# Merging the inverse in 64-row quadrants, moving the E products, and leading with the last channels

## The chip, the cores and the metric

The kernel runs on one core of a Trainium2 chip. The metric is the device time of one launch in microseconds. It was run seven times: median 1137.3 us, lowest 1134.52, highest 1139.42.

## What is computed

Two blocks in a row. The first is a linear recurrence over 768 tokens for 4 sequences of 8 heads, each head with a 40 by 40 state:

```python
for t in range(S):
    y[:, :, t] = einsum('bhd,bhde->bhe', rt, state)
    Sa = einsum('bhde,bhe->bhd', state, at)
    state = state * wt[:, :, None, :] - einsum('bhd,bhe->bhde', Sa, bt)
    state = state + einsum('bhd,bhe->bhde', vt, kt)
```

Its output, as 3072 tokens of 320 channels, goes through four experts that all tokens use. `p` is `domain_probs` divided by its row sum:

```python
for e in range(4):
    h = maximum(x @ w1[e], 0)            # 320 -> 1024
    out += p[:, e:e + 1] * (h @ w2[e])   # 1024 -> 320
```

All data are 32-bit floats.

## The kernel before

**The recurrence** is worked in chunks of 64 tokens. A *unit* is one chunk of two of the four sequences, so there are 12 x 2 = 24 units, and a tile holds the two sequences on its two halves of 64 partitions. Inside a unit the recurrence becomes a triangular system: `F` (L478) and `E` (L483) are products of the decayed keys with themselves, and the inverse of the identity minus the causal part of `F` is needed. The kernel inverts diagonal blocks of 32 by 32 (`substitute`, L511: VectorE turns the blocks into `M` and prepares them, GpSimd runs the substitution into `Z`), and `merge` (L563) joins the blocks into the 64 by 64 inverse `QT`: `pY` (L583) multiplies the block below the diagonal with one inverse, `pQ` (L595) multiplies the result with the other inverse, and ScalarE copies the sums from PSUM back (L589, L600). Both are written head by head with 32 x 32 tiles of TensorE: 16 matmuls each, for the quarters 1 and 3 or 0 and 2 of the partitions.

`within(q)` (L384) is a generator that makes everything of a unit that needs no state: decays `G` (transposes `pg`), tokens `NT` and `KT` (transposes `pNT`, `pKT`), causal scores `pc`, `F` and `E` (`pfe`: the F products and the E products stand in one pair of PSUM banks), `ET` (VectorE's causal copy of E, L493) and `pev`, the product of E with V, which ScalarE copies to `EV` (L504). `step(q)` (L603) does what needs the state: `prn`, `psat` (the product with the inverse `QT`, and its transpose), `pxr`, `pdy`. Nearly all of these are 64 x 64 quadrants of TensorE made by `quadrants` (L365), so they show as line 371. A 32-bit matmul is two weight loads and two matmuls in the trace, so a product of 16 matmuls is 32 matmul instructions.

**The experts** run on chunks of 256 tokens. `up` (L718) first multiplies the last 64 of the 320 channels with 64 x 64 tiles (L727, 8 matmuls of 256 columns), and then the first 256 channels with the full 128 x 128 array (L735, 8 matmuls). The second layer is a Strassen-like scheme of products (L842, 160 columns) over sums of tiles (`add_h`, L836, VectorE), and VectorE adds the scaled products to the output (L753). The pieces of `w1` stream in over the SP queue (L282).

**The order** of the work is written by hand in the loop at L1022, one turn for each unit `u`: the generators of unit u + 1's merge (`m`) and step (`s_next`), of the running step (`s`), and of the `within` of units u + 1 and u + 2 (`w_next`, `w`) are advanced a yield at a time, and `gap(n)` puts one or two pieces of the experts (from the list `todo`) between them as filler for TensorE. Turns with u < 5 are called early and have an order of their own. The TensorE stream of a late turn is, with the tile size in brackets: `pY` [32], L727 [64], L735 and L842 [128], `pQ` [32], F and E products `pfe`, `psat`, L727 [64], L735 and L842 [128], `pev`, `pxr`, L727 [64], L735, L842 and `pg` [128], `pdy`, L727 [64], L735, L842, `pNT`, `pKT` [128], `pc`, `prn` [64], and `pY` of the next unit.

**PSUM:** products of the recurrence take one bank at a time from five in turn (`big`, L72); the experts take from three (`mm`): two for the `ph` of an `up`, one for each product of the second layer. A bank is free again when its last reader is done.

Of the kernel before, what the change touches and what calls it, by code (L numbers as in the profile page):

```python
# [15 lines left out]
def kernel(  # L16
# [114 lines left out]
    def kept(name, shape, n, value=0.0, eng=nc.gpsimd, lo=0):  # L131
        tiles = []
        for i in range(n):
            t = const.tile(shape, FP32, name=f"{name}{i}")
            eng.memset(t[:, :, lo:shape[2]], value)
            tiles.append(t)
        turn = [0]

        def take():
            turn[0] += 1  # L140
            return tiles[(turn[0] - 1) % n]

        return take
# [15 lines left out]
    ETs = kept("ET", of_64, 1)  # L159
    EVs = kept("EV", of_64, 1, lo=D)  # L160
    QTs = kept("QT", of_64, 1)
    RHs = kept("RH", of_64, 1, lo=D)
    state = [kept(f"state{i}_", [P, NJ, 64], 1)() for i in range(B)]


    class Unit:
        pass
# [3 lines left out]
    def begin(u):  # L171
        q = Unit()
        q.u, q.c, q.bp = u, u // (B // 2), u % (B // 2)
        q.b = [2 * q.bp, 2 * q.bp + 1]
        q.start, q.end = q.c == 0, q.c == NC - 1
        q.n = {}
        units.append(q)
        return q
# [143 lines left out]
    def of_slot(x, s):  # L322

        return x.rearrange("p (j s) e -> p j s e", s=2)[:, :, s, :]
# [59 lines left out]
    def within(q):  # L384
# [93 lines left out]
        pf = quadrants(p, 0, BY_TOKENS, L, lambda j, s, i: (  # L478
            s, i ^ s, j, of_slots(q.AT, s, j, i), of_pairs(NT, s, j, i),
        ))  # L480
        if q.u == 0:
            p = banks("pe")
        pe = quadrants(p, NJ * L, BY_TOKENS, L, lambda j, s, i: (  # L483
            s, i, j, of_pairs(KT, s, j, i), of_slots(q.AT, s, j, i),
        ))
        q.F = sb.tile([P, H, L], FP32, name="F", tag="F", bufs=2)
        for s in range(2):
            nc.scalar.copy(out=of_slot(q.F[:], s), in_=pf[s])
        yield

        ET = ETs()
        for s in range(2):
# [18 lines left out]
    def substitute(q, eng, between=None):  # L511

        blocks = sb.tile([P, H, Q], FP32, name="blocks")
        for i in range(P // Q):
            move = nc.scalar.copy if i >= 2 else nc.vector.tensor_copy
            tc.keep_in_program_order(move(out=blocks[quarter(i)], in_=q.F[quarter(i), :, quarter(i % 2)]))  # L516
        M = sb.tile([P, Q, Q], FP32, name="M")
        cols = blocks[:].rearrange("p h c -> p c h")[:, :, None, :].to_broadcast([P, Q, 4, H])
        ins = nc.vector.transpose(out=M[:], in_=cols)  # L519
# [43 lines left out]
    def merge(q):  # L563


        Qc = sb.tile([P, H, Q], FP32, name="Qc", tag="q", bufs=2)
        QTc = sb.tile([P, H, Q], FP32, name="QTc", tag="q", bufs=2)
        tc.keep_in_program_order(nc.vector.transpose(out=dealt(Qc[:]), in_=q.Z))
        tc.keep_in_program_order(
            nc.vector.transpose(  # L570
                out=QTc[:].rearrange("p h r -> p (h r)"), in_=Qc[:].rearrange("p h c -> p (h c)"),
            )
        )
        q.QT = QTs()
        for i in range(P // Q):
            ins = nc.gpsimd.tensor_copy(out=q.QT[quarter(i), :, quarter(i % 2)], in_=QTc[quarter(i)])  # L576
            tc.keep_in_program_order(ins)
        yield

        py = big("pY")  # L580
        for h in range(H):
            for i in (1, 3):
                nc.tensor.matmul(  # L583
                    out=py[quarter(i - 1), h * Q:(h + 1) * Q], lhsT=q.F[quarter(i), h, 0:Q],
                    rhs=QTc[quarter(i), h, :], start=True, stop=True,
                )
        Y = sb.tile([P, H, Q], FP32, name="Yq")
        for i in (0, 2):
            nc.scalar.copy(out=Y[quarter(i)].rearrange("p h t -> p (h t)"), in_=py[quarter(i), 0:H * Q])  # L589
        yield  # L590

        pq = big("pQ")
        for h in range(H):
            for i in (0, 2):
                nc.tensor.matmul(  # L595
                    out=pq[quarter(i), h * Q:(h + 1) * Q], lhsT=Qc[quarter(i), h, :],
                    rhs=Y[quarter(i), h, :], start=True, stop=True,
                )
        for i in (0, 2):
            nc.scalar.copy(out=q.QT[quarter(i), :, quarter(1)], in_=by(pq[quarter(i), 0:H * Q], Q))  # L600
        yield

    def step(q, xT):  # L603
# [111 lines left out]
                lo = hi  # L715
        yield

    def up(k, xT, n, width):  # L718

        w1 = pieces[k]  # L720
        h = sb.tile([P, HF, 2 * P], FP32, name="hs", tag="hs", bufs=3)
        ph = [ps.tile([P, HF // 2, n], FP32, name="ph", tag="mm", bufs=3) for _ in range(2)]

        for f in range(HF // 2):
            for c in range(2):
                for i in range(2):
                    nc.tensor.matmul(  # L727
                        out=ph[i][half(c), f, :], lhsT=w1.last[part(i), f, half(c)],
                        rhs=xT[part(i), 2, :], start=(f == 0), stop=False,
                    )  # L730
        for i in range(2):
            for f in range(HF // 2):
                for g in range(2):
                    at = i * HF // 2 + f
                    nc.tensor.matmul(  # L735
                        out=ph[i][:, f, :], lhsT=w1.main[:, g, at * P:(at + 1) * P],
                        rhs=xT[:, g, :], start=False, stop=(g == 1 and f == HF // 2 - 1),
                    )
        for i in range(2):
            nc.scalar.activation(  # L740
                out=h[:, i * HF // 2:(i + 1) * HF // 2, 0:n], in_=ph[i][:], func=ACTF.Relu,
            )
        return h

    def scale(q, e, minus=False):
        return (minus_gate if minus else gate)[:, q.c, q.bp, e:e + 1]
# [16 lines left out]
    def mixture_of_unit(q):  # L763
# [1 line left out]
        hs, at = {}, 2 * E * q.u  # L765

        def ups(e):
            hs[e] = [up(at + 2 * e + x, q.xT, P, P) for x in range(2)]
            used(at + 2 * e + 2)
            if q.u == 0 and e + 2 < E:  # L770
                load_w2(e + 2)
# [44 lines left out]
    def mixture_of_chunk(qs, xT):  # L816
# [2 lines left out]
        at = 2 * E * (qs[0].c + 1)  # L819

        def ups(e, x):
            hs[e, x] = up(at + 2 * e + x, xT, 2 * P, P)
            used(at + 2 * e + x + 1)

        def of_h(e, s, x):
            return hs[e, x][:, :, s * P:(s + 1) * P]
# [60 lines left out]

        before = last[:]
        for e in range(E):
            todo.append(lambda e=e: ups(e, 0))  # L890
            if before:
                todo.append(before[0])
                todo.append(lambda e=e: ups(e, 1))
                todo.append(lambda e=e, then=before[1]: (then(), add_h(e)))
            else:
                todo.append(lambda e=e: (ups(e, 1), add_h(e)))
            second = down_2_at_end if (qs[0].end and e == E - 1) else down_2
            before = [lambda e=e: down_1(e), lambda e=e, second=second: second(e)]
        last[:] = before
# [9 lines left out]
    def mix(n):  # L909

        for piece in todo[:n]:
            piece()
            begin_later(3 if n > 1 else 6)
        del todo[:n]

    def run(gen, n=99):
        if gen is None:
# [104 lines left out]
    for u in range(1, NU):  # L1022
# [10 lines left out]
            run(sum_ops, sums_at.get(at, 0))  # L1033
            mix((1 if at in sparse else 2) if pieces is None else pieces)

        run(w_next)
        run(s, 1)
        gap(0)


        early = u < 5
        if early:
            run(s, 1)
        run(w, 1)
        run(s)
        if u == 1:
            mixture_of_unit(q)
# [28 lines left out]
        if not soon:  # L1076
            run(w, 1)
        if not early:
            run(s_next, 1)
        if not soon and u + 2 < NU:  # L1080
            substitute(units[u + 2], nc.gpsimd)
        run(w, 1)
        if u + 3 < NU:
            ws.append(within(units[u + 3]))
            run(ws[u + 3], 1)
# [41 lines left out]
```

## Time and profile before

| | |
|---|---|
| runs | median 1137.3 us of 7 (1134.52 to 1139.42) |
| the profiled execution's own time | 1134.52 us, of which its span is 1132.7 us |
| TensorE matmul, weight load busy | 96%, 85% of the span |
| VectorE, GpSimd, ScalarE busy | 67%, 42%, 30% |
| 16 DMA engines | 102 GB/s read and written over the span |
| granted TensorE clock | 0.95 up to 260 us, 1.00 from there on |
| TensorE busy in 0 to 260, 260 to 1005, 1005 to 1132.7 us | 229.4 of 260.0, 737.6 of 745.0, 123.6 of 127.7 us |

The units run up to about 1017 us; behind that only the experts' last pieces are left. From about 260 us on the loop is regular: a turn takes 43 to 45 us, so two turns (one chunk) take 87 to 88 us. A row of the groups gives the line, engine and operation, output and input tiles, their shapes and the count; then the busy time in us and the mean of one in ns; then the idle time of the engine just before them and what ended it. "PE" is TensorE's matmul, "PEld" its weight load. [...] successive matmuls overlap, so what a group of them costs is read from the start of the group to the start of the next.

### The profile page before, as it was taken

What the parts mean: (1) busy time and instruction counts of PE and PEld (TensorE: products, weight loads), DVE (VectorE), ACT (ScalarE), POOL (GpSimd) and SP (SyncE); (2) the same over time, 40 slices, a digit from 0 to 9 for tenths busy, and PEclk for the clock granted to TensorE, in tenths of its full rate; (3) what the DMA queues carried; (4) which work ended last, traced back from release to release, by engine and by line L of the source; (5) the groups of instructions that cost most, each with busy time, mean ns of one, the idle gap of its engine ahead of it and who ended that gap; (6) DMA issues with size and microseconds to landing.
All of it is one profiled execution on the core that took longest, in us unless ns stands there. A gap on an engine that the chain in (4) does not pass through costs nothing.

```text
span 1132.7 us, 39907 instructions
## 1 busy us (share of the span) xinstructions
PE 1090.6 (96%) x16868; PEld 961.9 (85%) x16868; DVE 759.5 (67%) x1553; ACT 338.2 (30%) x860; POOL 473.8 (42%) x1221
## 2 busy tenths in 40 slices
PE   6799997999999999999999999999999999999998
PEld 5677875888888989889898898888889899888887
DVE  8766657797667768668677677577686686553343
ACT  2323332333232232342332332332322323311110
POOL 4005626672724634625526427337346346340000
PEclk8899998999999999999999999999999999999999
DMA  7784643254263454444442543543444442231330
GB/s 116 204 252 129 136 98 79 70 129 102 76 153 80 111 129 114 110 118 104 107 121 74 134 103 82 142 102 88 128 113 92 117 111 64 76 90 55 105 93 12
DMA packets 268873, 122.27 MB, mean 108 GB/s; under 512 B 213736, under 2 KB 242072, under 8 KB 268696
## 3 DMA queue, kind: packets, MB, share of 16 engines
q1 hardware_dynamic: 265416, 119.12, 42.2%
q8 instruction: 133, 2.18, 0.8%
q10 hardware_dynamic: 3280, 0.61, 0.3%
q14 instruction: 44, 0.36, 0.1%
HBM read 111.79 MB, written 3.93 MB: 102 GB/s over the span
## 4 chain that ended last, share of the span: by engine, by line
PE 81%; DVE 6%; POOL 3%; SPq 3%; DMA 2%; issue 2%; ACT 2%; DVEq 0%; ACTq 0%; POOLq 0%
PE ph L735 27%; PE p L842 27%; PE ph L727 8%; PE pdy L371 3%; POOL Z L557 2%; PE pfe L371 2%; PE psat L371 2%; PE pxr L371 2%; PE prn L371 2%; SPq L711 1%; POOL Z L544 1%; PE pQ L595 1%; PE po L776 1%; PE pY L583 1%; PE pc L371 1%
## 5 line engine op out<-in xcount | busy, mean ns | idle before, releaser
L735 PE MATMUL ph<-xT,w1p 128*128 128x256 f32 (+1 forms) x1520 | 343.9, 379 | 0.4 <-issue 0.4
L735 PEld LDWEIGHTS ph<-xT,w1p 128*128 128x128 f32 x1520 | 274.0, 190 | 68.6 <-issue 29.0
L544 POOL TENSOR_TENSOR Z<-M,Z 128x62 f32<-128x62 f32 (+7 forms) x352 | 152.4, 433 | 366.0 <-DVE M L535 340.1
L557 POOL TENSOR_TENSOR Z<-Z 128x31 f32<-128x31 f32 (+7 forms) x704 | 249.4, 354 | 55.2
L836 DVE TENSOR_TENSOR a<-hs 128x512 f32<-128x512 f32 x220 | 154.4, 719 | 115.0 <-ACT hs L740 115.0
L740 ACT ACTIVATE hs<-ph 128x512 f32<-128x512 f32 (+1 forms) x208 | 115.8, 564 | 279.8 <-PE ph L735 279.0
L842 PE MATMUL p<-sums,a 128*128 128x160 f32 x1056 | 165.1, 299 | 0.0
L753 DVE SCALAR_TENSOR_TENSOR osb<-p,gate,osb 128x320 f32<-128x320 f32 (+1 forms) x243 | 108.0, 482 | 76.4 <-PE p L842 73.6
L842 PEld LDWEIGHTS p<-sums,a 128*128 128x128 f32 x1056 | 152.9, 190 | 2.3
L727 PE MATMUL ph<-xT,w1p 64*64 64x256 f32 (+1 forms) x1520 | 111.5, 379 | 5.1 <-issue 5.1
L842 PE MATMUL p<-w,a 128*128 128x160 f32 x704 | 103.1, 299 | 0.0
L842 PE MATMUL p<-w,hs 128*128 128x160 f32 x704 | 102.9, 299 | 0.0
L842 PEld LDWEIGHTS p<-w,hs 128*128 128x128 f32 x704 | 100.3, 190 | 2.2
L842 PEld LDWEIGHTS p<-w,a 128*128 128x128 f32 x704 | 98.1, 190 | 0.2 <-ACT hs L740 0.2
L576 POOL COPY QT<-QTc 32x256 f32<-32x256 f32 x96 | 50.1, 522 | 108.5 <-DVE QTc L570 97.9
L727 PEld LDWEIGHTS ph<-xT,w1p 64*64 64x64 f32 x1520 | 62.5, 133 | 17.9 <-issue 9.7
L519 DVE STREAM_TRANSPOSE M<-blocks 128x1024 f32<-128x1024 f32 x24 | 46.9, 1956 | 24.6 <-ACT blocks L516 24.4
L414 DVE RECIPROCAL gp<-gp 128x320 f32<-128x320 f32 x24 | 51.7, 2152 | 0.8
L504 ACT COPY EV<-pev 64x160 f32<-64x160 f32 x96 | 23.4, 286 | 67.7 <-PE pev L371 67.3
L626 ACT COPY SN<-prn 128x256 f32<-128x256 f32 x44 | 15.5, 370 | 91.6 <-DVE RH L621 89.2
L371 PE MATMUL pdy<-VC,k_tok 64*64 64x104 f32 (+1 forms) x768 | 41.3, 260 | 0.1
L667 ACT COPY RS<-pxr 64x256 f32<-64x256 f32 x88 | 32.3, 367 | 29.4 <-DVE SX L382 28.6
(148 smaller groups left out, 1351.7 us busy)
## 6 DMA issues: line engine op xcount, KB each, us to landing
w1p<-in_moe_w_dram SPq DMA_DIRECT2D x95, 512.0 KB
w1p<-in_moe_w_dram SPq DMA_DIRECT2D x190, 64.0 KB
w<-in_moe_w_dram SPq DMA_DIRECT2D x4, 1280.0 KB
sums<-in_moe_w_dram SPq DMA_DIRECT2D x9, 512.0 KB
natW<-in_w_dram SPq DMA_DIRECT2D x48, 80.0 KB
natB<-in_b_dram SPq DMA_DIRECT2D x48, 80.0 KB
natK<-in_k_dram SPq DMA_DIRECT2D x48, 80.0 KB
out_dram<-osb SPq DMA_DIRECT2D x46, 80.0 KB
```

The lines of the kernel that those rows point to most:

```text
L371: nc.tensor.matmul(out=p[row][half(col), lo + at * out_cols:lo + (at + 1) * out_cols], lhsT=lhsT, rhs=rhs, start=(n == 0), stop=(n == len( ...
L414: pin(nc.vector.reciprocal(out=gp[:], in_=gp[:]))
L519: ins = nc.vector.transpose(out=M[:], in_=cols)
L544: ins = eng.tensor_tensor(out=Z[:, 1:3, 0:n, j + 1:Q], in0=M[:, j:j + 2, None, j + 1:Q].to_broadcast([P, 2, n, m]), in1=Z[:, here, 0:n, j: ...
L557: eng.tensor_tensor(out=z[:, 0], in0=z[:, 0], in1=z[:, x], op=ALU.add)
L576: ins = nc.gpsimd.tensor_copy(out=q.QT[quarter(i), :, quarter(i % 2)], in_=QTc[quarter(i)])
L727: nc.tensor.matmul(out=ph[i][half(c), f, :], lhsT=w1.last[part(i), f, half(c)], rhs=xT[part(i), 2, :], start=(f == 0), stop=False,)
L735: nc.tensor.matmul(out=ph[i][:, f, :], lhsT=w1.main[:, g, at * P:(at + 1) * P], rhs=xT[:, g, :], start=False, stop=(g == 1 and f == HF // ...
L740: nc.scalar.activation(out=h[:, i * HF // 2:(i + 1) * HF // 2, 0:n], in_=ph[i][:], func=ACTF.Relu,)
L753: nc.vector.scalar_tensor_tensor(out=to, in0=p, scalar=sc, in1=to, op0=ALU.mult, op1=ALU.add)
L836: nc.vector.tensor_tensor(out=t[:], in0=x, in1=y, op=op)
L842: nc.tensor.matmul(out=p[:, n * HD:(n + 1) * HD], lhsT=a[:, f, :], rhs=b[:, f, :], start=(f == 0), stop=(f == HF - 1),)
```

## The change

Four things are changed.

- **The merge in quadrants.** `pY` and `pQ` are made by a new function `two_heads`: for each pair of heads and each half of 64 partitions one 64 x 64 matmul of 64 columns, so 8 matmuls each in place of 16. Both halves write the same PSUM bank. Of each product only the blocks on the diagonal are wanted; ScalarE copies them, four copies of 32 x 128 elements in place of two of 32 x 256. The other blocks have to be multiplied with zeros, so the block below the diagonal is copied to a tile of its own whose other quarters stay zero (`below`, two tiles in turn, two copies on GpSimd in each unit), and `Y` becomes a tile that is kept and was zeroed once. The copies to `below` stand in GpSimd's queue ahead of the substitution.
- **E products later.** From unit 7 on (`apart`) the F products are one stretch of `within`, with banks of their own, and the E products, with two more banks, the next; `ET` and `pev` follow one stretch later each. The loop runs the rest of `w_next` only after `w`'s next part. In TensorE's stream of a late turn the E products stand where `pev` stood, ahead of `pxr`, and `pev` stands ahead of `pdy`, behind `pg`.
- **The last channels lead.** `up` is split into `up_last` (L727) and `up_main` (L735). In late turns `lead()` issues the `up_last` of the next piece ahead of `psat`, where it stood behind it.
- `F` has one buffer in place of two.

In whole, TensorE has 8208 matmuls in place of 8592.

The diff, cut:

```diff
+    Ys = kept("Yq", [P, H, Q], 1)
+    belows = kept("below", [P, H, Q], 2)
+    EARLY = 5
+        q.apart = u >= EARLY + 2
...
-        if q.u == 0:
+        def copy_F():
+            q.F = sb.tile([P, H, L], FP32, name="F", tag="F", bufs=1)
+            for s in range(2):
+                nc.scalar.copy(out=of_slot(q.F[:], s), in_=pf[s])
+
+        if q.apart:
+            copy_F()
+            yield
+        if q.apart or q.u == 0:
             p = banks("pe")
         pe = quadrants(p, NJ * L, BY_TOKENS, L, lambda j, s, i: (
             s, i, j, of_pairs(KT, s, j, i), of_slots(q.AT, s, j, i),
         ))
-        q.F = sb.tile([P, H, L], FP32, name="F", tag="F", bufs=2)
-        for s in range(2):
-            nc.scalar.copy(out=of_slot(q.F[:], s), in_=pf[s])
-        yield
+        if not q.apart:
+            copy_F()
+            yield
...
+        q.below = belows()
+        for i in (1, 3):
+            tc.keep_in_program_order(nc.gpsimd.tensor_copy(out=q.below[quarter(i)], in_=q.F[quarter(i), :, 0:Q]))
...
-        py = big("pY")
-        for h in range(H):
-            for i in (1, 3):
-                nc.tensor.matmul(
-                    out=py[quarter(i - 1), h * Q:(h + 1) * Q], lhsT=q.F[quarter(i), h, 0:Q],
-                    rhs=QTc[quarter(i), h, :], start=True, stop=True,
-                )
-        Y = sb.tile([P, H, Q], FP32, name="Yq")
-        for i in (0, 2):
-            nc.scalar.copy(out=Y[quarter(i)].rearrange("p h t -> p (h t)"), in_=py[quarter(i), 0:H * Q])
-        yield
-        pq = big("pQ")
...
+        def two_heads(name, lhsT, rhs, to):
+            p = big(name)
+            for n in range(NJ):
+                for r in range(2):
+                    nc.tensor.matmul(
+                        out=p[half(r), n * 2 * Q:(n + 1) * 2 * Q], lhsT=lhsT[half(r), 2 * n:2 * n + 2, :],
+                        rhs=rhs[half(r), 2 * n:2 * n + 2, :], start=True, stop=True,
+                    )
+            for r in range(2):
+                for y in range(2):
+                    src = p[quarter(2 * r + y), 0:H * Q].rearrange("p (n two t) -> p n two t", two=2, t=Q)[:, :, y, :]
+                    nc.scalar.copy(out=of_slot(to[quarter(2 * r)], y), in_=src)
+
+        Y = Ys()
+        two_heads("pY", q.below, QTc, Y)
+        yield
+
+        two_heads("pQ", Qc, Y, q.QT[:, :, quarter(1)])
         yield
...
-        def ups(e, x):
-            hs[e, x] = up(at + 2 * e + x, xT, 2 * P, P)
-            used(at + 2 * e + x + 1)
+        def ups(e, x):
+            k, ph = at + 2 * e + x, []
+            def lead():
+                if not ph:
+                    ph.append(up_last(k, xT, 2 * P))
+            def piece():
+                lead()
+                hs[e, x] = up_main(k, xT, 2 * P, ph[0])
+                used(k + 1)
+            piece.lead = lead
+            return piece
...
+    def lead():
+        if todo and hasattr(todo[0], "lead"):
+            todo[0].lead()
...
-        run(w_next)
+        early = u < EARLY
+        run(w_next, 99 if early else 1)
         run(s, 1)
         gap(0)
-        early = u < 5
         if early:
             run(s, 1)
         run(w, 1)
+        if not early:
+            run(w_next)
         run(s)
...
         if not early:
+            lead()
             run(s_next, 1)
         if not soon and u + 2 < NU:
             substitute(units[u + 2], nc.gpsimd)
-        run(w, 1)
+        if early:
+            run(w, 1)
```

## Prediction, made before the changed kernel was run

> **What bounds the kernel now.** I read the page first, for the engine shares.
>
> ```profile
> span 1132.7 us, 39907 instructions
> PE 1090.6 (96%) x16868; PEld 961.9 (85%) x16868; DVE 759.5 (67%) x1553; ACT 338.2 (30%) x860; POOL 473.8 (42%) x1221
> ...
> q8 instruction: 133, 2.18, 0.8%
> ...
> PE 81%; DVE 6%; POOL 3%; SPq 3%; DMA 2%; issue 2%; ACT 2%; DVEq 0%; ACTq 0%; POOLq 0%
> ```
>
> TensorE is busy 96% of the span and holds 81% of the chain that ended last: a nanosecond off its stream is a nanosecond off the end wherever it doesn't wait. Next the waits of TensorE's matmuls, in the regular part (260 to 1005 us), to see what it waits for there:
>
> ```profile
> PE ph L727 <- issue: 3.3, 3, 1.4
> PE psat L371 <- issue: 2.5, 2, 1.3
> PE pY L583 <- DVE QTc L570: 1.3, 1, 1.3
> PE ph L735 <- issue: 0.4, 1, 0.4
> ```
>
> Hardly anything waits for another engine; what idling there is carries the label "issue", for which the profile shows no cause. The chain inside 801 to 806 us has one such hole, in the middle of a product:
>
> ```profile
> 801.21 1.09 PE pfe L371 x64
> 802.30 0.80 PE psat L371 x48
> 803.10 1.14 issue
> 804.25 0.42 PE psat L371 x11
> 804.67 1.16 PE ph L727 x15
> ```
>
> Last, TensorE's timeline, for what a group costs from its start to the next start (start, then duration):
>
> ```profile
> 747.18 0.67 PE L371 MATMUL prn<-ident,state 64*64 64x64 f32 x32
> 747.78 0.69 PE L583 MATMUL pY<-QTc,F 32*32 32x32 f32 x32
> 748.40 1.09 PE L727 MATMUL ph<-xT,w1p 64*64 64x256 f32 x16
> ...
> 757.43 0.69 PE L595 MATMUL pQ<-Yq,Qc 32*32 32x32 f32 x32
> 758.05 0.69 PE L371 MATMUL pfe<-NT,AT 64*64 64x64 f32 x32
> 758.56 0.65 PE L371 MATMUL pfe<-AT,KT 64*64 64x64 f32 x32
> 759.03 0.76 PE L371 MATMUL psat<-QT,RH 64*64 64x64 f32 x30
> ```
>
> A 64-column product that follows others of the same tile size costs 0.47 us (758.56 to 759.03). Ahead of a change of tile size it costs 0.60 (`prn` to `pY`), and the first one after a change 0.51 (`pfe` at 758.05).
>
> **Part 1, the merge in quadrants.** Starts of single matmuls show how a 0.47 us product runs: 8 rounds of four tiles, a round each 58.5 ns. `two_heads` also has 8 rounds (16 instructions on two tiles), so I take 0.47 us for it. Around `pY`, `prn` to L727 is now 0.60 + 0.62 = 1.22 us; with no change of tile size it is 0.47 + 0.47 = 0.94: 0.28 saved. Around `pQ`, which comes behind 128-wide work and still changes the tile size once, `pQ` and the first `pfe` are now 0.62 + 0.51 = 1.13; afterwards 0.51 + 0.47 = 0.98: 0.15 saved (the step from 128 to 32 and that from 128 to 64 both take 229 ns between starts). So 0.43 us a unit. From the seventh `pY` (264 us) on TensorE is the bound, for 18 units: 7.8 us. In the six units ahead, `pY` starts 0.05 to 0.15 us behind the end of `QTc` in four, so the chain through substitution sets the pace, and a shorter stream only waits longer: I take 0 (bounds: 6 x 0.43 = 2.6 saved; 6 x 0.4 = 2.4 lost to the copies below).
>
> [...] `two_heads` writes both row halves to one bank. [...] The row near to it is `pY` itself: its tiles stand in two row groups and write one bank, and the trace starts them in pairs 7 ns apart, a pair each 32 ns, about half of the 58.5 ns of a 64-column round whose row tiles have banks of their own; in turns a pair would take twice that. I go by the row[...].
>
> ScalarE: a copy of 32x256 takes 363 ns (L600), one of 64x160 286 ns (L504), so 0.8 ns an element; 32x128 is estimated at 0.26 us, and four with their 25 ns gaps at 1.14 us in place of 0.75. `Y` has about 10 us of experts' work as cover. `psat` needs all four copies of `pQ`: they end about 1.88 us behind `pQ`'s start, and TensorE gets to `psat` after `pQ`, F and the leading L727 at 0.47 + 0.51 + 0.9 = 1.9 us. That is just covered; if a copy of half the size cost the full 0.36, `psat` would wait 0.4 us, 7.4 us over 18 units. I take 0.05, so 1 us.
>
> GpSimd: two copies to `below`, about 0.39 us each like L576's median. They stand ahead of the substitution, where GpSimd waits for `M` anyway (340 us over 22 units): free. Without this cover they would cost 0.8 us a unit. `pY`'s new wait for `below` ended a unit before.
>
> **Part 2, E products later.** No product is added. E takes the place of `pev` behind 128-wide work, and `pev` joins `pdy`: by the prices above the sum moves by less than 0.03 us a unit. What goes is the hole. The page has 133 instruction packets of together 2.18 MB, 16 KB each; with 34,150 TensorE instructions (two for each of 16,868 matmuls, and 414 others) that is 256 instructions a packet. Five holes (at 455.4, 542.2, 629.1, 716.6 and 804.2 us) end where TensorE has started 14,274, 17,090, 19,906, 22,722 and 25,538 instructions: exactly 2,816, eleven packets, apart, while the code around them drifts. Each ends 1.4 to 1.6 us after a packet has landed. So TensorE runs out of instructions. Packets start on average 1.7 us after TensorE has reached the point 311 instructions ahead of the block, land 1 us later and serve 1.4 us later: 311 instructions must last about 4.1 us. In the stretch `pQ`, two `pfe`, two `psat`, L727 there are 352 in 3.6 us, and where a block ends in it, TensorE stops.
>
> [...] I price by the trace: segments from `pfe` to L735 take at least 2.96 us; at 537, 626, 713, 801 and 888 us they are 1.97, 1.11, 1.93, 1.66 and 0.39 us over it, and the L735 stretch at 454 is 0.72 over the usual: 7.8 us. Afterwards that stretch has 256 instructions with a slow L727 among them (2.9 us) and 128-wide work on both sides: 311 instructions last at least 6.2 us wherever a block ends in a regular turn. All 7.8 us should go, and nothing is late next at these places. One more hole, at 321.9 us, isn't at a block's end; I leave it in (it looks like the load of `w1p`).
>
> **Part 3, the lead.** `psat` to L735 and L727 to `psat` (0.16 + 0.20 us) take the place of L727 to L735 (0.31) and a step inside one tile size (0.04): nothing. The lead's second PSUM tile waits for VectorE's second read of the product `p75` (in the unit at 801 us it ends at 800.94; the lead comes at about 801.5). Behind a late lead are queued `psat`, and behind it ScalarE's copies to `blocks`, `M` and the substitution; each 0.1 us costs 0.1. Its piece of `w1p` must have landed 1 us earlier; such waits were 2.7 us in 7 cases, all inside changes of tile size, so 0 to 2 us, I take 0.
>
> **A wait to watch.** From `psat` to the next `pY` TensorE now needs about 30.8 us, and the chain `blocks`, `M`, substitution, `QTc` 29.4 to 29.8: `pY` starts 1.0 to 1.7 us behind `QTc`. With L727 (0.9) ahead of `psat` and E and `pev` both behind it, TensorE gets there 0.6 us sooner: 0.4 to 1.1 us of cover stay.
>
> **Sum.** Profiled execution: 1134.5 - 7.8 - 7.8 + 1 = 1119.9 us, 14.6 less. The median of the runs is 2.8 us above that execution, so 1137.3 - 14.6 = 1122.7; I say 1122.5.
>
> **Rivals.**
> - *Given back at `psat` and `pY`.* Half-size copies at full price (7.4 us), or the cover of `QTc` gone: 15.6 saved, 5 to 10 back: 1127 to 1133. Against it: the slope of two copy sizes.
> - *Blocks still run out* (the change doesn't do what it says, or new alignments meet new dense stretches, as in the early units): only part 1 counts, 1129 to 1131. Against it: the 6.2 us.
> - *More than that*: the early units gain their 2.6 us too, and the holes at 321.9 and 354 us shrink: 1116 to 1119.
> - *Slower: the shared bank.* Row tiles take turns in `two_heads`: 0.94 us more a unit, in the 18 late units and the six early ones, where `pY` and `pQ` lie on the chain, 22.5 us, less 15.6: 1144. It outweighs the gain from a delay of 0.33 us a product on (48 x 0.33 = 15.8).
>
> **Chances.** Forecast, 1119 to 1126: 0.62. Given back: 0.14. Blocks still run out: 0.09. More: 0.07. Shared bank: 0.05. Nothing moves, for causes I don't see: 0.03. The range 1117 to 1131 leaves out the last two and the edges. A measurement can tell about 0.2% (2.3 us): faster 0.92, within 0.03, slower 0.05.
>
> **What would show it.** `prn` to `pY` and `pY` to L727 at 0.47 us each; two neighbouring tiles of `pY` 7 ns apart and rounds of 58 ns (117 means turns). No "issue" rows ahead of L727 or `psat` from 400 us on. ScalarE's `QT<-pQ` at 0.26 us, and no wait of `psat` for it. `pY` still waiting for nothing. Turns of about 42.6 us, all alike. I am wrong if turns alternate again by over 0.5 us, or if `psat` or `pY` shows ScalarE, VectorE or GpSimd as what ended its wait.

## The result, and the profile after

| | before | after |
|---|---|---|
| median of the runs beside one another | 1135.88 us (34 runs) | 1129.64 us (13 runs, 1125.03 to 1131.98) |
| the profiled execution, its span | 1134.52, 1132.7 us | 1132.42, 1130.2 us |
| from the seventh `pY` to the 24th | 741.06 us | 733.00 us |

The ratio is 0.9937, with a 95% interval of 0.9923 to 0.9951: faster by 0.5 to 0.8%. The time lies inside the range that was stated (1117 to 1131), but outside the forecast's own 1119 to 1126, and the gain is less than half of what was forecast (6 to 7 us, not 14.6). So the question is where the rest went. The profiled execution of after is slower than all 13 others; its regular part is used below, its early part with care.

The page after has TensorE just as busy with 768 fewer matmul instructions, and six instruction packets fewer; the chain that ended last holds less of TensorE (72%, before 81%) and more of GpSimd and "issue":

```profile
span 1130.2 us, 38551 instructions
PE 1084.5 (96%) x16100; PEld 964.8 (85%) x16100; DVE 759.0 (67%) x1553; ACT 353.5 (31%) x956; POOL 498.5 (44%) x1272
...
q8 instruction: 127, 2.08, 0.8%
...
PE 72%; POOL 7%; DVE 6%; issue 3%; ACT 2%; DMA 1%; SPq 1%; DVEq 0%; POOLq 0%
```

The waits of TensorE's matmuls from 260 to 1005 us (engine, product and line, what it waited for; total us, times, longest) have lost `psat` and `pY`. The "issue" row ahead of the last channels (L727 before, L738 now) is larger, and `hs` is new:

```profile
PE ph L738 <- issue: 4.9, 4, 2.0
PE p L873 <- ACT hs L757: 1.0, 2, 0.7
```

TensorE's timeline in a steady turn (start, duration, group) shows what the merge brings. `prn`'s last part, `pY` and L738 start 0.49 and about 0.47 us apart, where `pY` alone cost 0.62 before a change of tile size:

```profile
748.71 0.67 PE L376 MATMUL prn<-ident,state 64*64 64x64 f32 x32
749.20 0.57 PE L599 MATMUL pY<-QTc,below 64*64 64x64 f32 x14
749.56 0.43 PE L738 MATMUL ph<-xT,w1p 64*64 64x256 f32 x2
749.61 0.22 PE L599 MATMUL pY<-QTc,below 64*64 64x64 f32 x2
749.67 1.03 PE L738 MATMUL ph<-xT,w1p 64*64 64x256 f32 x14
```

**Where the time went, from the seventh to the 24th `pY` (17 turns).** I cut TensorE's stream at its changes between 128-wide and smaller tiles, take for each kind of stretch the shortest one of the regular part, and count what every other one has over it.

| | before | after | difference |
|---|---|---|---|
| shortest stretches around `pY`, `pQ`, `pxr`, `pdy`, summed over a turn | 11.84 us | 11.34 us | -0.50 a turn, -8.4 |
| stops where an instruction block ends | 7.8 us | 0 | -7.8 |
| stretches with `pQ`, F, `psat` and L727, over the least, at 275 to 420 us | 3.0 us | 7.9 us | +4.9 |
| products that wait for `hs` | 0.3 us | 4.4 us | +4.1 |
| `psat` behind the copies of `pQ` | 0 | 0.9 us | +0.9 |
| `pY` behind `QTc`, and small ones | 1.7 us | 0 | -1.7 |
| sum | | | -8.0 (measured -8.06) |

So from the seventh to the 24th `pY` 18 us were saved and 10 were given back. **The theory after this reading (A):** both savings are as large as forecast; the lead and ScalarE's longer queue give back half. Rivals: (B) the merge itself is worth less; (C) the early units, which in this profile are 6 us later, lose it; (D) the stops in the lead are instruction fetch again.

The lead's stops come at 325.49, 370.51 and 416.26 us, each behind the first two of its 16 instructions, that is at the second PSUM tile, and not at a block's end. VectorE's timeline ahead of the second stop:

```profile
364.52 0.93 DVE L228 STREAM_TRANSPOSE G<-rawW 128x256 f32<-128x256 f32 x2 [4.69 <-DMA rawW<-in_w_dram]
...
369.01 0.51 DVE L773 SCALAR_TENSOR_TENSOR osb<-p,gate,osb 128x320 f32<-128x320 f32 x1
...
370.04 0.37 DVE L773 SCALAR_TENSOR_TENSOR osb<-p,minus_gate,osb 128x160 f32<-128x160 f32 x1
```

and TensorE's:

```profile
367.94 0.59 PE L738 MATMUL ph<-xT,w1p 64*64 64x256 f32 x2
370.51 1.55 PE L738 MATMUL ph<-xT,w1p 64*64 64x256 f32 x11 [1.98 <-issue]
```

VectorE stood 4.7 us for the load of `rawW`; the second read of `p75` (`minus_gate`) is queued behind what it did late, and ends at 370.41. TensorE goes on 0.10 us later. At the other two places VectorE had stood 7.0 us for `rawW` and 3.9 us for `rawA`; the read ends at 325.39 and 416.16, and the lead goes on at 325.49 and 416.26. The seven such stops in the traces of experiments 2, 5 and 11 end 0.10 us behind that read too. So the label "issue" hid a wait for a PSUM tile.

### The profile page after: what moved, and what is told of

It is laid out like the page before. It is cut to its first block, busy times and chain, and to the rows that moved or that the text cites. A ratio compares the mean times of both kernels' runs of the same rounds, so it can differ in the third digit from the quotient of the medians.

```text
span 1130.2 us, 38551 instructions
## 1 busy us (share of the span) xinstructions
PE 1084.5 (96%) x16100; PEld 964.8 (85%) x16100; DVE 759.0 (67%) x1553; ACT 353.5 (31%) x956; POOL 498.5 (44%) x1272
## 4 chain that ended last, share of the span: by engine, by line
PE 72%; POOL 7%; DVE 6%; issue 3%; ACT 2%; DMA 1%; SPq 1%; DVEq 0%; POOLq 0%
PE p L873 25%; PE ph L752 25%; PE ph L738 7%; POOL Z L572 4%; PE pdy L376 3%; POOL Z L559 3%; PE psat L376 2%; PE po L796 2%; PE pxr L376 1%; PE prn L376 1%; DVE M L534 1%; PE pQ L599 1%; PE pfe L376 1%; PE pev L376 1%; PE pc L376 1%
## 5 line engine op out<-in xcount | busy, mean ns | idle before, releaser
L752 PE MATMUL ph<-xT,w1p 128*128 128x256 f32 (+1 forms) x1520 | 342.7, 378 | 1.7 <-issue 1.7
L752 PEld LDWEIGHTS ph<-xT,w1p 128*128 128x128 f32 x1520 | 273.4, 190 | 62.9 <-issue 25.3
L572 POOL TENSOR_TENSOR Z<-Z 128x31 f32<-128x31 f32 (+7 forms) x704 | 256.5, 364 | 55.2
L559 POOL TENSOR_TENSOR Z<-M,Z 128x62 f32<-128x62 f32 (+7 forms) x352 | 144.4, 410 | 135.5 <-DVE M L550 109.7
L531 POOL COPY below<-F 32x256 f32<-32x256 f32 x48 | 24.9, 519 | 223.0 <-ACT F L489 221.3
L738 PE MATMUL ph<-xT,w1p 64*64 64x256 f32 (+1 forms) x1520 | 110.5, 377 | 4.9 <-issue 4.9
L873 PE MATMUL p<-w,a 128*128 128x160 f32 x704 | 106.0, 301 | 1.2 <-ACT hs L757 1.0
L738 PEld LDWEIGHTS ph<-xT,w1p 64*64 64x64 f32 x1520 | 65.3, 133 | 13.6 <-issue 9.1
L583 DVE STREAM_TRANSPOSE Qc<-Z 128x256 f32<-128x256 f32 x24 | 15.1, 628 | 46.9 <-POOL Z L572 46.6
```

Source lines behind the costliest of these rows:

```text
L559: ins = eng.tensor_tensor(out=Z[:, 1:3, 0:n, j + 1:Q], in0=M[:, j:j + 2, None, j + 1:Q].to_broadcast([P, 2, n, m]), in1=Z[:, here, 0:n, j: ...
L572: eng.tensor_tensor(out=z[:, 0], in0=z[:, 0], in1=z[:, x], op=ALU.add)
L738: nc.tensor.matmul(out=ph[i][half(c), f, :], lhsT=w1.last[part(i), f, half(c)], rhs=xT[part(i), 2, :], start=(f == 0), stop=False,)
L752: nc.tensor.matmul(out=ph[i][:, f, :], lhsT=w1.main[:, g, at * P:(at + 1) * P], rhs=xT[:, g, :], start=False, stop=(g == 1 and f == HF // ...
L873: nc.tensor.matmul(out=p[:, n * HD:(n + 1) * HD], lhsT=a[:, f, :], rhs=b[:, f, :], start=(f == 0), stop=(f == HF - 1),)
```

## The experiments

Each ratio is against the kernel before, run on the same chip, with its 95% interval.

**1. The merge alone.** The kernel before with `two_heads` and `below`, and

```diff
-        q.F = sb.tile([P, H, L], FP32, name="F", tag="F", bufs=2)
+        q.F = sb.tile([P, H, L], FP32, name="F", tag="F", bufs=1)
```

> The kernel before with the merge in quadrants alone (and one buffer of F in place of two[...]). Theory A (each part is worth what was forecast in the regular part, and half of it is given back at three places: the lead, ScalarE's copies ahead of hs, the early units): the stream is 7.8 us shorter, the 'issue' holes at a block's end stay (other places), p<-w,a waits for hs 3 us in all, early units lose up to 4: 1 to 5 us less than before. Theory B (the merge itself is worth half of what was forecast, the rest is right): 4 us less, and no waits of p<-w,a for hs. Theory C (nothing given back by the merge): 7.8 us less.

1131.68 us, 0.9955 (0.9937 to 0.9972): 5.1 us less. No product waited for `hs`, against theory A, and only two stops at a block's end were left in the regular part (0.95 us at 279.6, which the profile puts down to a load of `rawV`, and 1.27 at 887.9), though nothing was done against these. What gave back here is another thing: from `pQ` to L737 takes at least 3.83 us, where the same products take 3.36 in experiment 11, because `psat` now waits for the four copies of `pQ`.

Why so few stops are left is shown in part. Two turns of before hold some 2,832 instructions, 16 more than eleven blocks, so the end of a block creeps slowly through the same dense place. Here two turns hold some 2,705, 145 more than ten blocks, and an end comes back to a place only after 14 turns (the two stops are 18,944 instructions, 74 blocks, apart). But some ends fall as late in the stretch and don't stop. That the wait of `psat` lets the fetch catch up there is not shown: experiment 11 stops at the same two ends (280 and 892 us), and its `psat` doesn't have that wait.

**2. All but the merge** (`pY` and `pQ` as before, no `below`).

> The kernel after with the old merge (16 matmuls of 32x32 tiles, two copies, no copies to below): E products later and the lead are left. Theory A: the five holes at a block's end go (7.8 us) and the lead waits at 322 to 420 us for VectorE's second read of p75 (5 to 6 us back): 2 to 3 us less than before. Theory B (the holes were worth 7.8 and the lead costs nothing): 7.8 us less than before. No p<-w,a waits for hs over 0.5 us in all, by both.

1138.32 us, 1.0004 (0.9992 to 1.0017): no gain. In its profile the block-end stops are gone and the lead stops at 325, 371 and 417 us (1415, 3997 and 2131 ns over the least), as A says; from the seventh `pY` to the 24th it needs 738.0 us, 3.1 less than before. Two turns still hold some 2,831 instructions, so here it is not another rhythm of the blocks that took the stops away. That its median is not 2 to 3 us lower isn't explained by this. Two things on record go with it: its profile has the seventh `pY` at 269.6 us (264.4 before), and its 22 runs spend 41.0 us in the median at half the granted clock, against 34.0 in before's beside them (from the mean granted clock).

**3. All but the lead**

```diff
         if not early:
-            lead()
             run(s_next, 1)
```

> The kernel after without the lead: the last channels stand behind psat again. Theory A: the three stops inside the lead at about 325, 370 and 416 us (1.3, 2.0 and 1.1 us, 7.7 us with the slow matmuls behind them) shrink by the 1 us that psat now covers each, and the slow ones with them: 4 to 6 us less than after. Rival (these stops are instruction fetch, and would come elsewhere): within 1.5 us of after, with 'issue' stops in other stretches.

1137.22 us, 0.9999 (0.9982 to 1.0016): all of the gain is gone. The three stops did vanish, but the other turns cost more (43.4 to 43.8 us from 400 us on, where after mostly takes 42.7 to 42.9). ScalarE's and TensorE's timelines:

```profile
757.81 1.10 ACT L606 COPY QT<-pQ 32x128 f32<-32x128 f32 x4 [3.49 <-PE pQ L599]
```

```profile
757.08 0.62 PE L599 MATMUL pQ<-Yq,Qc 64*64 64x64 f32 x14
...
758.17 1.41 PE L376 MATMUL psat<-QT,RH 64*64 64x64 f32 x31
759.37 0.26 PE L376 MATMUL psat<-RH,QT 64*64 64x40 f32 x5
```

The four copies end at 758.91, 1.83 us behind `pQ`'s start; `psat` begins at 758.17, its first half takes 1.20 us instead of 0.50, and the stretch from `pQ` to L752 at least 3.82 us instead of 2.93. So the lead, which I had priced at nothing, is worth 0.9 us a turn, because with E gone from there it is the only cover of these copies. My expectation looked at three turns and forgot the other fourteen.

**4. The old merge in the units below 7.**

```diff
+        if not q.apart:
+            py = big("pY")
...
+            return
```

> The kernel after, but the units below 7 keep the old merge (and no copies to below): the regular part is that of after. Theory A (the six units ahead of the seventh pY lose by the merge: four copies on the chain of each pY and pQ, two copies ahead of the substitution): pY of unit 7 starts 3 to 5 us earlier than in after, and the time is 3 to 5 us less. Rival (the early part is later only because of where instruction blocks end, or by chance of one execution): within 1.5 us of after.

1133.30 us, 0.9961 (0.9945 to 0.9978): no gain over after. Its `pY` of unit 7 starts at 312.96 us, after's at 313.16. So nothing here speaks for theory C, that the early units lose by the merge what is missing; but nothing clears the merge either, since the runs of this kernel spend 42.9 us in the median at half clock and those of after 31.6.

**5. The lead from unit 9 on.**

```diff
-            lead()
+            if u >= 9:
+                lead()
```

> The kernel after, with the lead only from the turn of unit 9 on; the three turns before it have the last channels behind psat, as without the lead. Theory A (in those three turns the lead waits for VectorE's second read of p75, because VectorE itself waits for the loads of rawW and rawA): the stops at 325, 370 and 416 us (excess 1.9, 4.2 and 1.6 us) go, each of the three turns pays the 0.9 us that psat waits for the four copies of pQ, and the half clock behind 370 us goes: 4 to 5 us less than after, 1125. Rival (an instruction fetch that moves): stops of the same sum elsewhere, within 1.5 us of after.

1128.81 us, 0.9914 (0.9891 to 0.9938). In the profile the three stretches are 1.05, 2.07 and 1.19 us over the least instead of 1.90, 4.17 and 1.63: the stops are gone but for 0.58 us at 367, and what is left is mostly the 0.9 us that `psat` pays without the lead. No "issue" stop came up elsewhere (against D), but the time does not come back in the regular part. From the seventh to the 24th `pY` it takes 732.65 us, after 733.00: the three stretches gain 3.4 us, and against that the one at 275 us, without the lead too, takes 1.0 more, products wait 1.4 us more for `hs` (5.8 over the least) and `pY` 0.5 for `QTc`. That the profile as a whole is 4.5 us shorter than after's comes from the early units (seventh `pY` at 266.3 us, after 270.4), which this edit leaves alone. The interval overlaps that of after, so the medians can't tell the two kernels apart either.

**6. SN copies behind the Yq copies.** ScalarE's timeline of after, at a turn where a product waits:

```profile
492.04 0.26 ACT L606 COPY Yq<-pY 32x128 f32<-32x128 f32 x1 [1.39 <-PE pY L599]
496.83 0.65 ACT L638 COPY SN<-prn 128x256 f32<-128x256 f32 x2 [4.54 <-DVE RH L633]
497.49 0.80 ACT L606 COPY Yq<-pY 32x128 f32<-32x128 f32 x3
498.31 1.08 ACT L757 ACTIVATE hs<-ph 128x512 f32<-128x512 f32 x2
```

`SN` waits 4.5 us for VectorE's `RH`; three copies and then `hs` stand behind it.

```diff
-            for s in range(2):
-                nc.scalar.copy(out=SN[:, s], in_=psn[s])
+            def copy_SN():
+                for s in range(2):
+                    nc.scalar.copy(out=SN[:, s], in_=psn[s])
+            q.copy_SN = copy_SN
+            if q.u < EARLY + 1:
+                copy_SN()
...
             run(m, 1)
+            if u + 1 < NU:
+                units[u + 1].copy_SN()
```

> The kernel after, with ScalarE's two SN copies issued behind the four Yq copies from unit 6 on (in after three of the four Yq copies stand behind SN, which waits for VectorE's RH, and hs stands behind them). Theory A (p<-w,a waits for hs because those copies are in front of it): hs starts 0.8 us earlier, the waits of p<-w,a for hs (4.1 us of the weight loads in 13 turns; 3.2 us over the least of that stretch) fall under 1 us, and the time is 2 to 3 us less than after. Rival (the wait is set by VectorE's RH itself, or the turn is set by the chain through the substitution, so that it comes back as a wait of pY for QTc): within 1 us of after.

1130.36 us, 0.9909 (0.9879 to 0.9939). The profiled execution (1135.02 us) is the slowest of its six; its lead stops for 2.3 us ahead of 416 us, where after's stops for 1.1. In the stretch behind `pY` the waits for `hs` fell from 3.2 us to 0.01, and seven of its turns take 42.47 to 42.62 us, where after's steady ones, but one, take 42.7 to 42.9. But the stretch behind `pxr` now waits 5.6 us for `hs` (1.2 in after). There VectorE stands for a raw load, and ScalarE's `RS` and `hs` stand behind it:

```profile
649.45 0.71 DVE L228 STREAM_TRANSPOSE VT<-rawV 128x512 f32<-128x512 f32 x1 [5.32 <-DMA rawA<-in_a_dram]
650.09 0.74 DVE L387 COPY_PREDICATED SX<-mask_up,pxr 128x256 f32<-128x256 int32 x2
```

```profile
650.53 1.50 ACT L685 COPY RS<-pxr 64x256 f32<-64x256 f32 x4 [11.34 <-DVE SX L387]
```

So the queue order was one cause, as expected, and a late raw load is another. The queue order is not enough alone: experiments 1 and 3 have the same copies in the same order but no lead, and no product waits for `hs` there, while 2 and 11 have the lead and such waits (1.7 and 8.8 us over the least). The waits come with the lead; how it brings them is not shown.

**7. Both.** The edits of 5 and 6.

> The late lead and the late SN copies together in the kernel after. Theory A: both gains add, 6 to 8 us less than after, 1122 to 1124, and ahead of both other kernels. Rival (a shorter turn runs into the chain blocks, M, substitution, QTc): pY waits for QTc, and the sum is no better than the better of the two.

1130.40 us, 0.9921 (0.9894 to 0.9948): the gains don't add in the medians. The stretch from the seventh to the 24th `pY` is the shortest of these kernels in its profile, 730.98 us, but what is left (3.0 us for `hs` behind `pxr`, 1.0 us of `pY` for `QTc` at 356) takes most of it. Its seventh `pY` comes at 270.8 us, as late as in after.

**8. The kernel before, its instruction blocks shifted by half a block.**

```diff
         gap(0)
+        if u == 9:
+            idle = big("idle")
+            for _ in range(32):
+                ins = nc.tensor.matmul(out=idle[0:Q, 0:Q], lhsT=ident[0:Q, 0:Q], rhs=ident[0:Q, 0:Q], start=True, stop=True)
+                tc.keep_in_program_order(ins)
```

> The kernel before with 32 matmuls of 32x32 (some 128 instructions, half a block) put in at unit 9, at about 430 us; they are of no use to the output. Theory A (the five stops at 455, 542, 629, 717 and 804 us come where a block of 256 instructions ends inside the dense stretch): they leave these turns or move to another place in them, and stops come in the other turns, again 2,816 instructions apart. Rival (they belong to the turn of every second unit, by a load of w1p or a bank that comes late there): they stay at the same matmuls, 1 to 2 us later. The time says little here: within 5 us of before.

The stops left their turns. They now come at 592.90, 682.32, 771.19 and 946.85 us, where TensorE has started 18,625, 21,442, 24,257 and 29,889 instructions: 2,817, 2,815 and 2 x 2,816 apart, and in the other turns. Divided by 256 these counts leave 193 or 194, as the five of before do (194): it is the same point of a block. The one at 592.9, in the middle of a product:

```profile
590.04 0.65 PE L727 MATMUL ph<-xT,w1p 64*64 64x256 f32 x6
592.90 0.80 PE L727 MATMUL ph<-xT,w1p 64*64 64x256 f32 x9 [2.21 <-issue]
```

That these stops belong to the instruction blocks is shown. (The single time, 1147.66 us, is 8.6 above this chip's median of before, more than the 5 expected; the 32 matmuls and larger stops are in it.)

**9. Raw loads earlier.** The cause behind the lead's stops is a raw load that lands late, so I moved these loads up.

```diff
+        if u + 3 < NU and not early:
+            for move in load_raw(begin(u + 3), "WA"):
+                tc.keep_in_program_order(move(nc.sync))
         gap(1)
...
-            piece()
             begin_later(3 if n > 1 else 6)
+            piece()
```

> The kernel after with the raw loads of a unit issued earlier: those of W and A (eight) ahead of the experts' pieces of the third gap's predecessor instead of behind them, some 10 us earlier and ahead of two loads of w1p in SP's queue, those of V and R one piece earlier. Theory A (what the lead and hs wait for in the end are raw loads that land late: VectorE stands at G<-rawW for 7.0 and 4.7 us, at AT<-rawA for 3.9, at VT<-rawV for 18 us in 8 turns, with p75's second read, RH and SX behind it in its queue): VectorE's waits for rawW and rawA go, the stops in the lead at 325, 370 and 416 us (7.7 us over the least) go to under 1.5, and the waits for hs shrink to under 2 us: 6 to 9 us less than after, 1121 to 1124. Rival (VectorE is simply behind with its own work there): the stops stay, within 1.5 us of after. Second rival (the loads of w1p behind the raw ones now come late): L738 or L752 waits for w1p, slower than after by some us.

1153.10 us, 1.0115 (1.0090 to 1.0141): the second rival. The largest wait of TensorE, and SP's timeline:

```profile
PE ph L738 <- DMA w1p<-in_moe_w_dram: 11.3, 6, 2.3
```

```profile
494.06 2.14 SPq L210 DMA_DIRECT2D rawW<-in_w_dram  x4
496.25 1.93 SPq L210 DMA_DIRECT2D rawA<-in_a_dram  x4
498.28 1.62 SPq L287 DMA_DIRECT2D w1p<-in_moe_w_dram  x3
```

Each of these issues takes SP about 0.5 us, and they go one after the other: eight raw loads ahead of `w1p` are 4.1 us by which `w1p` is issued later. And VectorE waited for `rawW` 15 times, 73 us in all: its transposes now stand 2.1 to 3.5 us behind the issue of the last of these loads, where in after's late turns it is mostly 24 to 27. The run shows what the SP queue's order costs; it doesn't show what loads in time would have brought.

**10. The same with the SN copies last.**

> The earlier raw loads, and the SN copies behind the Yq copies. Theory A: with VectorE no longer held by rawV, hs has neither RS nor Yq in front of it that wait; no wait for hs over 0.3 us, 1 to 2 us less than with the earlier loads alone. Rival: the chain through the substitution is next, pY waits for QTc, no gain over the earlier loads alone.

1151.18 us, 1.0103 (1.0073 to 1.0133). The interval overlaps that of experiment 9, so nothing follows beyond it.

**11. Merge and lead, the E products where they were.** Experiment 1 with `up_last`, `up_main` and `lead()`.

> The kernel before with the merge and the lead, the E products left where they were. It tells what moving them is worth once the merge and the lead are there. Theory A (the dense stretch is then pQ, F, E, L727, psat: some 380 instructions in 3.4 us, and instruction blocks run out in it as before): 'issue' stops of 1 to 2 us at five or six block ends, 2,7xx instructions apart, 5 to 8 us more than after, so about no gain over the merge alone. Rival (the four copies of pQ make psat wait long enough that blocks keep up, and E in front of it only fills that wait): within 2 us of after, and moving the E products is worth nothing.

1138.17 us, 0.9984 (0.9961 to 1.0006). The waits of TensorE's matmuls:

```profile
PE p L863 <- ACT hs L747: 5.6, 12, 0.5
PE ph L728 <- issue: 3.7, 3, 1.8
```

So moving E is worth about 5 us once merge and lead are there (0.9984 against 0.9937), as A says, but not by the blocks alone: two stops at block ends, not the five or six expected (1.0 and 1.6 us over the least, at 280 and 892), the lead's stops, and `hs` late by 0.46 us in each of twelve turns (8.8 us over the least in all). It looks as if where E stands sets when `psat` and what follows on ScalarE and VectorE come, against the experts' `hs`; this was not tried apart.

**12. TensorE kept busy in the early waits.** In the traces of before and after the stretches of half granted clock are 3.41, 10.24 and 17.07 us long, one, three and five times 3.413 us, but for those at the span's end. Over 14 executions of after, each us at half clock (27 to 38 us in all, from the mean granted clock) goes with 0.45 us more time. The edit adds to experiment 5, ahead of `pY` and of unit 3's `pxT`:

```diff
+    def fill(p, n):
+        for _ in range(n):
+            nc.tensor.matmul(out=p[:, 0:P], lhsT=ident[:], rhs=ident[:], start=True, stop=True)
```

> The late lead, with 26 matmuls of 128x128 that nobody reads, put where TensorE waits in the early units (3, 12 and 3 ahead of pY of units 3, 4 and 5; 8 ahead of unit 3's pxT): TensorE waited there 1.0, 3.4, 1.1 and 2.2 us. Theory A (a window of 3.41 us in which TensorE has idled for some 2 us is followed by one at half clock, and a us at half clock costs about 0.45 us: this is why single executions of one kernel lie 7 us apart): the half-clock windows at 183 to 204 us go, 7 to 10 us of half clock less over the runs' median than the 28 of the late lead, and 2 to 4 us less time: 1125 to 1127. Rival (the clock follows how dense the work is over longer times, or the fill delays pY by as much): half-clock time as before within 3 us, time within 1.5 us of the late lead.

1132.23 us, 0.9943 (0.9924 to 0.9962). The half-clock time fell from 28.2 to 24.8 us in the median, the time did not: that it goes along with the time from run to run doesn't make it a cause that can be taken away like this.

**Together**, in ratios to before:

| | without lead | with lead |
|---|---|---|
| merge, E in place | 0.9955 | 0.9984 |
| merge, E later | 0.9999 | 0.9937 |
| old merge, E later | not run | 1.0004 |

The parts of the change don't add. Each of E and the lead alone makes the merged kernel slower or no better, and only both together take it back to a gain. Whether the whole change (0.9923 to 0.9951) is any better than the merge alone (0.9937 to 0.9972) the intervals can't tell. The fastest versions (the late lead 0.9914, the SN copies last 0.9909) beat both kernels in their medians, but can't be told from after by the intervals.

## Why the prediction was half right

- **Part 1, the stream** (0.43 us a unit, 7.8 us): right. 0.33 us around `pY` (forecast 0.28) and 0.17 in the other three stretches together (0.15 around `pQ`, and nearly nothing for the moves of E and the lead), 8.4 us over 17 turns. The shared bank cost nothing here: in the turn at 749 us `pY`'s tiles start in pairs 6 ns apart, a pair each 58 ns (in turns it would be 117), and from `pY`'s start to L738's it is one product of 0.47 us. No trace here shows row halves that take turns, as the rival had it. Theory B is out.
- **Part 2, the blocks** (7.8 us): right. The shift shows that the stops belong to the blocks, and experiment 2 that they go without any change of the merge. No stop at a block's end is left from the seventh `pY` on. The count of 311 instructions and 4.1 us by which a fetch runs ahead is an estimate from before's packets (133 of 16,384 bytes, 1.09 us from start to landing in the mean) and was not tested.
- **ScalarE's copies of `pQ`**: the copy takes 0.26 us, all four end 1.83 us behind `pQ`'s start (forecast 1.88), and `psat` loses 0.9 us in all (1 was taken). Right.
- **Part 3, the lead: "nothing".** This step failed, in both directions. I had named its wait, VectorE's second read of `p75`, and priced it from the one unit at 801 us, where the read ends 0.6 us early. At 322 to 420 us VectorE is late by its raw loads, and the lead pays: 4.9 us more than before. I had also had the sign of it in hand: the stop at 321.9 us of before, which I took for "the load of `w1p`", is the same wait (the read ends at 321.79, VectorE having stood 8.73 us for `rawW`). A lead that comes 1 us earlier had to make it longer. On the other side, without the lead the change has no gain at all (experiment 3). My sum for the copies did lean on the leading L727, but I never priced part 3 as that cover. What the three stops cost in the end is less than their 4.9 us: with the lead put off past them (experiment 5) the regular part is only 0.35 us shorter, since other waits take their place.
- **ScalarE: "`Y` has about 10 us of experts' work as cover".** True for `Y`, and the wrong question. I asked who waits for the copies, and not who is queued behind them: `hs` is, 0.8 us later by three copies behind an `SN` that waits for VectorE. 4.1 us, of which the reordering of experiment 6 shows 3.2 to be this queue, in kernels with the lead. What is left behind `pxr` comes with late raw loads.
- **GpSimd and the early units**: taken as 0 within -2.6 to +2.4. In after's profile they are 6 us later; at `pY` of unit 1 it is 3.7, of which two half-clock windows (42.9 and 70.2 us), which before's profile doesn't have there, make most. In the profiles of experiments 1 and 5, without these windows, the seventh `pY` is at 266.3 us against 264.4: 1.9 us later, inside the bounds (both have one 6.8 us window at half clock there, before's has 10.2). That fits what the regular part gains and the medians don't show (8.06 against 6.2 us). In the traces of all experiments but the eighth the seventh `pY` is later than before's, at 265.5 to 271.9 us, also with the old merge there (269.6 in 2 and 4). The cause stays open; the one buffer of `F`, which all of them have, was never tried by itself.
- **`QTc`'s cover** (0.4 to 1.1 us): measured 0.6 to 0.97 in 14 of the last 17 turns. Right.

Before's lines for the stop at 321.9 us (VectorE, then TensorE):

```profile
318.13 0.93 DVE L223 STREAM_TRANSPOSE G<-rawW 128x256 f32<-128x256 f32 x2 [8.73 <-DMA rawW<-in_w_dram]
...
321.41 0.38 DVE L753 SCALAR_TENSOR_TENSOR osb<-p,minus_gate,osb 128x160 f32<-128x160 f32 x1
```

```profile
321.89 1.09 PE L727 MATMUL ph<-xT,w1p 64*64 64x256 f32 x14 [1.43 <-issue]
```

Of the signs that the prediction named, the late turns came: from 448 us on they take 42.5 to 43.1 us, but for one of 43.9 and the last, shorter one. The turns ahead of that are not alike (42.7, 44.4, 46.7 and 44.1 us), and the "issue" stop at 416 us lies behind the 400 us from which there was to be none.

The sum was to be 15.6 saved less 1 given back; from the seventh `pY` on it is 17.9 saved (with 1.7 of small ones) less 9.9, and the early units take some 2 more. That the time still lies in the stated range is luck as far as the mechanism goes: the range was wide enough for a loss at places that were priced at nothing. The rival *given back at `psat` and `pY`* had the right size (5 to 10 us) and time (1127 to 1133) at the wrong place: it is given back at L738 and at `hs`. The table says where the time went, not what each loss would give if it were gone: neither experiment 5 nor 6 brought its loss back in the regular part (732.65 and 737.23 us, after 733.00), and both together brought 2.0 (730.98). What stays open: why the early units are later, how much of the medians of experiments 2 and 7 that explains, and what the raw loads would bring if they landed in time.

## What to carry to other kernels

When a step is moved up, its price is set by the worst unit as well as by a steady one: look for the latest arrival of each thing it needs over the whole trace, and follow "issue" stops to the tile at which they happen. When copies are added on an engine, ask first what is queued behind them and what the one in front of them waits for (ScalarE's `hs` at 498.31 us stood behind an `SN` that waited 4.54 us and three copies). A stop that is taken away gives its time back only where nothing else is late next. And parts of a change that cover each other's waits have no separate prices: what one takes away (E from in front of `psat`) another must put back (the lead), so cost them in the order in which TensorE meets them.

## What the runs showed of the hardware

The granted clock of TensorE in stretches of after (length, TensorE's busy time, clock, DMA), around the stop at 370 us:

```profile
366.00:370.50 4.50, 2.53 (x58) 1.00 0.72 122
370.50:374.00 3.50, 3.49 (x78) 0.51 0.83 235
```

A stop of 1.98 us was followed by 3.41 us at half clock (370.54 to 373.95 us). This stretch is 4.2 us over the least; what is left beside the stop, some 2.2 us (an estimate: 4.17 less 1.98), goes with the half clock. The stops of 1.3 and 1.1 us at 325 and 416 were not followed by one.

In before and in after all stretches of half clock begin whole steps of 3.413 us apart (in after those at 196.46 and 370.54 us are 51 steps apart). I divided the traces of the fourteen kernels, from about 40 to 1000 us, at these steps. Each of the 31 steps at full clock in which TensorE stood for 1.92 us or more (by the modelled ends of its matmuls) was followed by half clock, and none of the 3,682 in which it stood for less than 0.79 us was; of these, before and after have 5 (1.95 to 3.37 us) and 528. In between both happened: the step at 173.57 us of before, with 1.69 us, was not followed by half clock, and the one at 192.4 us of experiment 4, with about 1.8 us, was.
